# Attention steps in pairs, value scaling in pieces, masks on two engines: one change to a kernel for banded attention and a gated feed-forward block

## The chip, the cores and the metric

The kernel runs on one core of a Trainium2 chip. TensorE (PE) multiplies matrices and its weight loads (PEld) run beside it. VectorE (DVE), ScalarE (ACT) and GpSimd (POOL) do the elementwise work; POOL cannot read the accumulators (PSUM), which PE writes. Transfers are issued from the queues of POOL and SyncE (SP). Each engine takes its instructions in order, so one that waits holds up all that stand behind it. The metric is the device time of one execution in microseconds (us), as the median of several runs.

## The reference

Four batches, eight heads, 768 positions, head width 64. Each query sees the 95 positions before it, itself and the first 8 positions; the scores get a linear bias with one slope per head. The attention output goes through a feed-forward block with 512 inputs and 1536 hidden columns.

```python
scores = scale * np.matmul(q, k.transpose(0, 1, 3, 2))
is_global = pos[None, :] < int(n_global)                  # 8
is_local = (rel >= 0) & (rel < int(n_local))              # 96
bias = -slopes[:, None, None] * dist[None, :, :]
scores = np.where(is_global | is_local, scores + bias[None], -1e9)
a = np.exp(scores - scores.max(-1, keepdims=True))
attn = np.matmul(a / (a.sum(-1, keepdims=True) + 1e-09), v)
x = attn.transpose(0, 2, 1, 3).reshape(B * S, H * D)      # 3072 x 512
g = x @ w_gate
out = (g * (1.0 / (1.0 + np.exp(-g))) * (x @ w_val)) @ w_out
```

## The kernel before

**Attention** is worked for two heads at a time: `Pair(b, hp)` is batch `b` (0 to 3) and head pair `hp` (0 to 3). A pair has six steps, which this text calls by short names. *tr*: 24 PE transposes of q and k into PSUM (`trq`, `trk`), copies on ACT into `qT` and `kT`, and a small copy that puts the 8 global keys into each chunk of `kT` (DVE for batch 0, POOL for the others). *sc0, sc1, sc2*: a third of the keys each, matmuls into two PSUM banks (`scA`, `scB`), two exponentials on ACT into `at`, and two multiplications of `at` with the mask `masks` (DVE for batch 0, POOL for the others). *va0, va1*: half of the queries each; matmuls of `at` with ones (`den`) and with v (`num`), then on DVE a transpose of `den` to `dT`, a reciprocal `dR`, a transpose back that spreads it to `rb`, and last the product with `num` into `xT` (on DVE for batch 0, the "fast" form; else ACT copies `num` to `ns` and POOL multiplies). va0 needs the masked sc0 and sc1; va1 needs sc1 and sc2.

**Feed-forward.** The 3072 tokens are 8 blocks `t` of 384; two blocks are one batch. A block has 12 column groups `f`, and each of these three groups of PE work: gate (`gps`, 4 matmuls), value (`vps`, 4 matmuls) and, from block 1 on, a quarter of an output tile of the block before (`ops`, 3 matmuls). ACT takes the tanh of `gps` into `th`, DVE makes `sl` of `th` and `gps`, then `hT` of `vps` and `sl`. `gps` and `vps` take three PSUM banks in turn (tags x0, x1, x2), `ops` one (o0), which ACT empties into `osb` after every fourth quarter; attention takes four (a0 to a3) in turn. With three banks, the value group of `f+1` uses the bank that `sl` of `f` must have read, and the gate group of `f+2` that of `hT` of `f`.

**What sets the order.** There is no scheduler: each engine's instructions stand in the order in which the code issues them. Half of batch 0 (tr, sc0, sc1, va0 of four pairs) is done ahead, the "prologue". Then the last loop walks the groups and, by a quota of steps for each amount of feed-forward work, calls the next attention step of `plan` between two groups. `second(b)` lists sc2 and va1 of a batch, `first(b)` tr, sc0, sc1 and va0. 80 steps are placed in this way. `loads` says before which group POOL issues the transfers of a later batch: q and k four heads at a time (`load_qk`), v by chunk (`load_v_rest`). After the last block, 12 quarters of `ops` remain.

Of the kernel before, what the change touches and what calls it, by code (L numbers as in the profile page):

```python
# [37 lines left out]
def kernel(  # L38
# [119 lines left out]

    attn_tags = ["a0", "a1", "a2", "a3"]
    pro_tags = ["a0", "a1", "a2", "a3", "x0", "x1", "x2", "o0"]  # L160
    state = {"tags": pro_tags, "n": 0}

    def bank(name, dt=FP32, cols=512):
        tags = state["tags"]
# [5 lines left out]
    def make_masks(h, c0, c1):  # L170
        nc.scalar.activation(
            out=masks[:, h, c0:c1], in_=dist[:, c0:c1], func=AF.Exp, scale=-slopes[h])

    class Pair:
        def __init__(self, b, hp):
# [3 lines left out]
        def transposes(self):  # L179
            b, hp = self.b, self.hp  # L180
            trq = bank("trq", FP16, S)
            trk = bank("trk", FP16, S)
            for st, tr in ((qst[b], trq), (kst[b], trk)):
                for j in range(J):
                    for hi in range(2):
                        nc.tensor.transpose(  # L186
                            tr[64 * hi:64 * hi + 64, 128 * j:128 * j + 128],
                            st[:, 2 * hp + hi, D * j:D * j + D], ident)
            self.qT = sb2.tile([128, S], FP16, name="qT", tag="qT", bufs=NP)
            self.kT = kTs[hp]  # L190
            nc.scalar.copy(
                out=self.qT.rearrange("r (p j) -> r p j", j=J),
                in_=trq.rearrange("r (j p) -> r p j", j=J))
            k3 = self.kT.rearrange("r (c m) -> r c m", m=128)
            t3 = trk.rearrange("r (j p) -> r p j", j=J)
            for c0, c1, n in ((0, 6, KC), (6, 7, S - 6 * KC)):
                nc.scalar.copy(
                    out=k3[:, c0:c1, NG:NG + n].rearrange("r c (p j) -> r c p j", j=J),
                    in_=t3[:, 20 * c0:20 * c0 + (c1 - c0) * (n // J), :].rearrange(
                        "r (c p) j -> r c p j", c=c1 - c0))  # L200
            (nc.vector if b == 0 else nc.gpsimd).tensor_copy(  # L201
                out=k3[:, :, 0:NG],
                in_=k3[:, 0, NG:2 * NG].unsqueeze(1).broadcast_to([128, NCH, NG]))

        def scores(self, bk, mul_eng):
# [10 lines left out]
                        lhsT=self.kT[r, 128 * c:128 * c + 128],  # L216
                        rhs=self.qT[r, q0:q0 + n], start=True, stop=True)
            for hi in range(2):
                keep = f"at{hi}{bk}b{hp}" if bk == 1 else f"at{hi}{bk}"
                at = sb2.tile([128, BANK], FP16, name="at", tag=keep, bufs=1 if "b" in keep else 2)  # L220
                nc.scalar.activation(out=at, in_=sc[hi][:, 0:BANK], func=AF.Exp, scale=scale)  # L221
                self.at[hi, bk] = at
            for hi in range(2):
# [10 lines left out]
        def values(self, half, fast):  # L234
# [11 lines left out]
            for dst, ones_side in ((den, True), (num, False)):  # L246
# [13 lines left out]
            nc.vector.transpose(dT[:, 0:n_q], den[:, 0:n_q])  # L260
            nc.vector.reciprocal(
                out=dR[:, 0:nb], in_=dT[:, 0:n_q].rearrange("p (n i) -> p n i", i=32)[:, :, 0])
            nc.vector.transpose(  # L263
                rb[:, 0:n_q].rearrange("p (n i) -> p n i", i=32),
                dR[:, 0:nb].unsqueeze(2).broadcast_to([128, nb, 32]))
            dst = xT[:, hp, b * S + lo:b * S + hi_q]
            if fast:
                nc.vector.tensor_mul(dst, num[:, 0:n_q], rb[:, 0:n_q])  # L268
            else:
                ns = sb2.tile([128, 416], FP32, name="ns", tag="ns")  # L270
                nc.scalar.copy(out=ns[:, 0:n_q], in_=num[:, 0:n_q])  # L271
                nc.gpsimd.tensor_mul(dst, ns[:, 0:n_q], rb[:, 0:n_q])  # L272


    hTs = {}
# [3 lines left out]
    def gate_or_val(t, f, which):  # L279
        if f == 0 and which == 0:  # L280
            hTs[t] = sb2.tile([128, NFF, TB], FP16, name="hT", tag="hT")
        w = (wg, wv)[which]
        dst = ps.tile([128, 512], FP32, name="gv"[which] + "ps", tag=f"x{gv.get('n', 0) % 3}")
        gv["n"] = gv.get("n", 0) + 1
        for c in range(NC):
            nc.tensor.matmul(  # L286
# [15 lines left out]

    def out_part(t, i, part):
        if part == 0:
            ops_t[0] = ps.tile([128, 512], FP32, name="ops", tag="o0")
        ops = ops_t[0]
        for f in range(3 * part, 3 * part + 3):
            nc.tensor.matmul(  # L308
                ops, lhsT=hTs[t][:, f, 128 * i:128 * i + 128], rhs=wo[:, f, :],
                start=(f == 0), stop=(f == NFF - 1))  # L310
        if part == 3:
            osb = sb2.tile([128, DM], FP32, name="osb", tag="osb")
            nc.scalar.mul(out=osb, in_=ops, mul=0.5)  # L313
            r0 = TB * t + 128 * i
            nc.sync.dma_start(out=out[r0:r0 + 128, :], in_=osb)
# [43 lines left out]
    for t in range(4 + 2 * (NP - 1)):  # L359
        for hp in range(NP):  # L360
            s = t - 2 * hp
            if 0 <= s < 4:
                early(hp, s)
                if s == 1 and hp + 1 < NP:
                    make_masks(2 * hp + 2, 0, BANK)
                    make_masks(2 * hp + 3, 0, BANK)
# [2 lines left out]
    state["tags"] = attn_tags  # L369
    state["n"] = 0  # L370

    def second(b):
        steps = []
        for kind, hp in ((0, 0), (0, 1), (1, 0), (0, 2), (1, 1), (0, 3), (1, 2), (1, 3)):
            p = pairs[b, hp]
            steps.append((lambda p=p: p.values(1, b == 0)) if kind else
                         (lambda p=p: p.scores(2, nc.vector if b == 0 else nc.gpsimd)))
        return steps

    def first(b):  # L380
        keyed = []
        for hp in range(NP):
            p = pairs[b, hp]
            keyed += [(4 * hp, p.transposes),
                      (4 * hp + 2, lambda p=p: p.scores(0, nc.gpsimd)),
                      (4 * hp + 3, lambda p=p: p.scores(1, nc.gpsimd)),
                      (4 * hp + 5, lambda p=p: p.values(0, False))]
        return [fn for _, fn in sorted(keyed, key=lambda x: x[0])]


    plan = [((0,), second(0)), ((1,), first(1)), ((2, 3), second(1) + first(2)),
            ((4, 5), second(2) + first(3)), ((6,), second(3))]

    loads = {13: [lambda: load_qk(1, 4, 8)]}
    for c in range(4, NCH):
        loads[14 + c] = [lambda c=c: load_v_rest(1, c)]
    for b in range(2, B):
        base = 24 * (b - 2) + 26
        loads[base] = [lambda b=b: (stage(b), load_qk(b, 0, 4))]
        loads[base + 2] = [lambda b=b: load_qk(b, 4, 8)]  # L400
        for c in range(NCH):
            loads[base + 3 + c] = [lambda b=b, c=c: load_v_rest(b, c)]


    NT = TOK // TB
# [8 lines left out]
    for blocks, steps in plan:  # L414
# [4 lines left out]
    owed = 0.0  # L419
    seen = set()  # L420
    for t, f, work, fn in groups:
        if (t, f) not in seen:
            seen.add((t, f))
            for ld in loads.get(NFF * t + f, []):
                ld()
        fn()
        owed += work * quota.get(t, 0.0)
        while owed >= 1.0 and todo:
            todo[0][1].pop(0)()
            owed -= 1.0  # L430
            if not todo[0][1]:
                assert t <= todo[0][0]
                todo.pop(0)
                owed = 0.0
    assert not todo
    for i in range(3):
        for part in range(4):
            out_part(NT - 1, i, part)
# [35 lines left out]
```

## Time and profile before

| what | value |
|---|---|
| runs shown: median (lowest to highest) | 285.01 us (284.49 to 285.19) |
| the profiled execution: time, span | 286.0 us, 284.2 us |
| granted TensorE clock | 0.999 |
| DMA queue of POOL | 14.20 MB, 44.3% of 16 engines |

The profiled execution took 1.0 us more than the median of the runs shown; its span, from the first to the last instruction, is 1.8 us less than its own time. All rows below are of this execution, with times from the start of the span. A row of the timeline gives start, duration, engine, line, operation, output and inputs, the number of instructions, and in brackets how long the engine sat idle before it and what ended that. A row of the waits says which line of which engine waited for what: us in total, times, the longest. A row by groups ends with busy time and mean ns, then the idle time ahead of them.

### The profile page before, as it was taken

What the parts mean: (1) busy time and instruction counts of PE and PEld (TensorE: products, weight loads), DVE (VectorE), ACT (ScalarE), POOL (GpSimd) and SP (SyncE); (2) the same over time, 40 slices, a digit from 0 to 9 for tenths busy, and PEclk for the clock granted to TensorE, in tenths of its full rate; (3) what the DMA queues carried; (4) which work ended last, traced back from release to release, by engine and by line L of the source; (5) the groups of instructions that cost most, each with busy time, mean ns of one, the idle gap of its engine ahead of it and who ended that gap; (6) DMA issues with size and microseconds to landing.
All of it is one profiled execution on the core that took longest, in us unless ns stands there. A gap on an engine that the chain in (4) does not pass through costs nothing.

```text
span 284.2 us, 5710 instructions
## 1 busy us (share of the span) xinstructions
PE 258.3 (91%) x2240; PEld 141.4 (50%) x2240; DVE 161.3 (57%) x333; ACT 145.2 (51%) x305; POOL 149.9 (53%) x178
## 2 busy tenths in 40 slices
PE   1687999799988999999999999899999999999973
PEld 1464455444544555545545555555545555555531
DVE  1377589945545576465466666445565676556500
ACT  4788343275654645755754546466655443332211
POOL 8984550067486787873665687694366451000000
PEclk9999999999999999999999999999999999999999
DMA  9999999317070169970000199950100101001011
GB/s 106 169 166 189 203 205 186 26 9 142 3 78 0 39 92 181 97 79 2 37 37 2 39 163 131 87 68 0 39 37 1 39 37 39 24 12 40 38 74 74
DMA packets 45531, 21.28 MB, mean 75 GB/s; under 512 B 28256, under 2 KB 42432, under 8 KB 45504
## 3 DMA queue, kind: packets, MB, share of 16 engines
q0 software_dynamic: 41504, 14.20, 44.3%
q1 hardware_dynamic: 4000, 6.72, 6.5%
q8 instruction: 17, 0.28, 0.4%
q14 instruction: 10, 0.08, 0.1%
HBM read 28.58 MB, written 6.29 MB: 123 GB/s over the span
## 4 chain that ended last, share of the span: by engine, by line
PE 61%; POOL 13%; DMA 13%; issue 7%; ACT 3%; DVE 1%; POOLq 0%; ACTq 0%; DVEq 0%
PE ops L308 20%; PE gps L286 16%; PE vps L286 16%; DMA wo<-in_moe_w_out_dram 4%; POOL at L228 4%; DMA wv<-in_moe_w_val_dram 4%; DMA vS<-in_v_dram 3%; POOL at L232 3%; PE den L250 3%; PE scA L214 3%; PE num L250 2%; DMA qst<-in_q_dram 2%; POOL vS L123 2%; PE trq L186 1%; ACT osb L313 1%
## 5 line engine op out<-in xcount | busy, mean ns | idle before, releaser
L295 DVE SCALAR_TENSOR_TENSOR sl<-th,gps 128x384 f32<-128x384 f32 x96 | 53.0, 552 | 78.3 <-ACT th L293 77.8
L286 PE MATMUL gps<-xT,wg 128*128 128x384 f16 x384 | 80.1, 331 | 2.1 <-DVE xT L268 1.8
L286 PE MATMUL vps<-xT,wv 128*128 128x384 f16 x384 | 79.6, 331 | 1.1 <-DVE sl L295 1.1
L293 ACT ACTIVATE th<-gps 128x384 f32<-128x384 f32 x96 | 47.5, 494 | 64.1 <-PE gps L286 62.6
L308 PE MATMUL ops<-wo,hT 128*128 128x512 f16 x288 | 76.6, 380 | 2.1 <-ACT osb L313 2.1
L299 DVE TENSOR_TENSOR hT<-vps,sl 128x384 f16<-128x384 f32 x96 | 53.2, 554 | 10.0 <-PE vps L286 1.5
L232 POOL TENSOR_TENSOR at<-at,masks 128x432 f16<-128x432 f16 x48 | 47.1, 1001 | 8.1 <-ACT at L221 7.6
L286 PEld LDWEIGHTS <-wg 128*128 128x128 f16 x384 | 35.5, 99 | 31.5 <-issue 3.1
L286 PEld LDWEIGHTS <-wv 128*128 128x128 f16 x384 | 35.9, 98 | 27.0 <-issue 4.2
L272 POOL TENSOR_TENSOR xT<-ns,rb 128x384 f16<-128x384 f32 x24 | 24.0, 998 | 44.7 <-DVE rb L263 28.1
L308 PEld LDWEIGHTS <-hT 128*128 128x128 f16 x288 | 26.0, 98 | 27.3 <-issue 4.9
L221 ACT ACTIVATE at<-scA 128x432 f16<-128x432 f32 x48 | 25.4, 529 | 17.7 <-PE scB L214 16.5
L250 PE MATMUL den<-at,ones 128*64 128x216 f16 (+6 forms) x288 | 19.6, 241 | 6.5 <-POOL at L228 3.2
L221 ACT ACTIVATE at<-scB 128x432 f16<-128x432 f32 x48 | 25.4, 530 | 0.0
L271 ACT COPY ns<-num 128x384 f32<-128x384 f32 x24 | 11.5, 479 | 25.4 <-PE num L250 24.1
L228 POOL TENSOR_TENSOR at<-at,masks 128x432 f16<-128x432 f16 x24 | 23.6, 1005 | 1.5 <-ACT at L221 1.4
L123 POOL DMA_DIRECT2D vS<-in_v_dram x24 | 21.7, 905 | 3.3 <-issue 2.3
L313 ACT ACTIVATE osb<-ops 128x512 f32<-128x512 f32 x24 | 14.4, 599 | 17.0 <-PE ops L308 17.0
L250 PEld LDWEIGHTS <-ones 128*64 128x64 f16 x288 | 12.3, 113 | 19.9 <-issue 14.5
L214 PE MATMUL scA<-qT,kT 64*128 64x216 f16 (+2 forms) x112 | 18.0, 264 | 2.8 <-DVE kT L201 2.7
L260 DVE STREAM_TRANSPOSE dT<-den 128x384 f32<-128x384 f32 x32 | 18.4, 576 | 3.0 <-PE den L250 3.0
L263 DVE STREAM_TRANSPOSE rb<-dR 128x384 f32<-128x384 f32 x32 | 18.5, 578 | 2.7
(32 smaller groups left out, 180.9 us busy)
## 6 DMA issues: line engine op xcount, KB each, us to landing
out_dram<-osb SPq DMA_DIRECT2D x24, 256.0 KB, 2.0
vS<-in_v_dram POOLq DMA_DIRECT2D x20, 120.0 KB, 5.0
qst<-in_q_dram POOLq DMA_DIRECT2D x5, 384.0 KB, 5.4
kst<-in_k_dram POOLq DMA_DIRECT2D x5, 384.0 KB, 6.6
wg<-in_moe_w_gate_dram POOLq DMA_DIRECT2D x4, 384.0 KB, 10.0
wv<-in_moe_w_val_dram POOLq DMA_DIRECT2D x4, 384.0 KB, 10.9
wo<-in_moe_w_out_dram POOLq DMA_DIRECT2D x3, 512.0 KB, 14.2
qst<-in_q_dram POOLq DMA_DIRECT2D x6, 192.0 KB, 6.5
```

Of the source, the lines that this page charges most:

```text
L123: nc.gpsimd.dma_start(out=vSs[b][NG:NG + n, c, :, :], in_=v[b, :, KC * c:KC * c + n, :].rearrange("h p d -> p h d"))
L214: nc.tensor.matmul(sc[hi][:, col:col + n], lhsT=self.kT[r, 128 * c:128 * c + 128], rhs=self.qT[r, q0:q0 + n], start=True, stop=True)
L221: nc.scalar.activation(out=at, in_=sc[hi][:, 0:BANK], func=AF.Exp, scale=scale)
L228: mul_eng.tensor_mul(a2, a2, m[:, WIN:2 * WIN].unsqueeze(1).broadcast_to([128, 2, WIN]))
L232: mul_eng.tensor_mul(at, at, m[:, o:o + BANK])
L250: nc.tensor.matmul(dst[r, o:o + n], lhsT=ones if ones_side else vSs[b][:, c, 2 * hp + hi, :], rhs=self.at[hi, cb][:, col:col + n], start=( ...
L272: nc.gpsimd.tensor_mul(dst, ns[:, 0:n_q], rb[:, 0:n_q])
L286: nc.tensor.matmul(dst[:, 0:TB], lhsT=w[:, c, 128 * f:128 * f + 128], rhs=xT[:, c, TB * t:TB * t + TB], start=(c == 0), stop=(c == NC - 1))
L293: nc.scalar.activation(out=th, in_=dst[:, 0:TB], func=AF.Tanh, scale=0.5)
L295: nc.vector.scalar_tensor_tensor(out=sl, in0=th, scalar=1.0, in1=dst[:, 0:TB], op0=AluOp.add, op1=AluOp.mult)
L299: nc.vector.tensor_mul(hTs[t][:, f, :], dst[:, 0:TB], gv["sl"])
L308: nc.tensor.matmul(ops, lhsT=hTs[t][:, f, 128 * i:128 * i + 128], rhs=wo[:, f, :], start=(f == 0), stop=(f == NFF - 1))
```

## The change

In words, part by part:

- **Pairs.** `plan` now holds lists of steps that are issued directly one behind the other: sc0 with sc1 of the same pair of heads, sc2 of two pairs, va1 of two pairs, tr of two pairs or va0 with tr. Only the steps in block 0 (`single`) and some va0 stay alone. The 80 steps stand in 48 places. `owed` starts at 0.8, and at 0.4 for each new list.
- **Pieces.** The DVE work of a va step is queued as functions in `later`: `invert` (dT and dR), `spread` (rb, and POOL's product) and, for batch 0, `scale_num`. One is run after each feed-forward group; all that are left are run ahead of the next attention place and at each block's start. In the prologue all run at once.
- **Masks.** For batches 1 to 3, sc0 and the sc2 of even pairs multiply on DVE, sc1 and the sc2 of odd pairs on POOL.
- **kT.** Batch 0's two large copies go from ACT to DVE; the copy of the global keys is on DVE for all batches.
- **Banks and buffers.** In block 0 gate and value take four banks (o0 too, which nothing else uses yet). The last three output tiles take a0, a1 and o0. All `at` tags have four buffers.
- **Loads.** q and k of batch 1 (heads 4 to 7) before group 10 instead of 13; of batch 2 before 23 and 24 instead of 26 and 28; of batch 3 before 38 and 40 instead of 50 and 52 (groups are counted 12 to a block); v follows.

```diff
-            (nc.vector if b == 0 else nc.gpsimd).tensor_copy(
+            nc.vector.tensor_copy(
...
+            def invert():
+                nc.vector.transpose(dT[:, 0:n_q], den[:, 0:n_q])
+                nc.vector.reciprocal(
...
+            def spread():
...
+                if not fast:
+                    nc.gpsimd.tensor_mul(dst, ns[:, 0:n_q], rb[:, 0:n_q])
...
+            later.append(invert)
+            later.append(spread)
             if fast:
-                nc.vector.tensor_mul(dst, num[:, 0:n_q], rb[:, 0:n_q])
+                later.append(scale_num)
...
-            ops_t[0] = ps.tile([128, 512], FP32, name="ops", tag="o0")
+            tag = ["a0", "a1", "o0"][i] if t == TOK // TB - 1 else "o0"
...
+    def sc(b, hp, bk):
+        on_vector = b == 0 or bk == 0 or (bk == 2 and hp % 2 == 0)
...
+    def second(b):
+        return [[sc(b, 0, 2), sc(b, 1, 2)], [sc(b, 2, 2), sc(b, 3, 2)],
+                [va(b, 0, 1), va(b, 1, 1)], [va(b, 2, 1), va(b, 3, 1)]]
+    def first(b):
+        return [[tr(b, 0), tr(b, 1)],
+                [sc(b, 0, 0), sc(b, 0, 1)], [sc(b, 1, 0), sc(b, 1, 1)],
+                [va(b, 0, 0), tr(b, 2)], [sc(b, 2, 0), sc(b, 2, 1)],
+                [va(b, 1, 0), tr(b, 3)], [sc(b, 3, 0), sc(b, 3, 1)],
+                [va(b, 2, 0)], [va(b, 3, 0)]]
+    def both(b):
+        x, y = second(b), first(b + 1)
+        return x[:3] + [y[0], x[3]] + y[1:]
+    single = [[sc(0, 0, 2)], [sc(0, 1, 2)], [va(0, 0, 1)], [sc(0, 2, 2)],
+              [va(0, 1, 1)], [tr(1, 0)], [sc(0, 3, 2)], [va(0, 2, 1)], [va(0, 3, 1)], [tr(1, 1)]]
+    plan = [((0,), single), ((1,), first(1)[1:]), ((2, 3), both(1)),
+            ((4, 5), both(2)), ((6,), second(3))]
...
+        if f == 0:
+            run_later(len(later))
+        if t == 1 and f == 0:
+            state["x"] = ["x0", "x1", "x2"]
         fn()
+        run_later(1)
...
-            todo[0][1].pop(0)()
+            run_later(len(later))
+            for step in todo[0][1].pop(0):
+                step()
```

Three places show what moves; the numbers behind the names only tell buffers apart. On DVE in block 0, the rows that follow a va1 step of batch 0, before:

```order
L299 TENSOR_TENSOR hT_480<-vps_651,sl_649 128x384
L260 STREAM_TRANSPOSE dT_679<-den_658 128x384
L261 RECIPROCAL dR_680<-dT_679 128x12
L263 STREAM_TRANSPOSE rb_681<-dR_680 128x384
L268 TENSOR_TENSOR xT_96<-num_657,rb_681 128x384
L295 SCALAR_TENSOR_TENSOR sl_693<-th_691,gps_686 128x384
```

and now:

```order
L317 TENSOR_TENSOR hT_480<-vps_740,sl_738 128x384
L313 SCALAR_TENSOR_TENSOR sl_778<-th_776,gps_771 128x384
L269 STREAM_TRANSPOSE dT_768<-den_747 128x384
L270 RECIPROCAL dR_769<-dT_768 128x12
L317 TENSOR_TENSOR hT_480<-vps_782,sl_778 128x384
L275 STREAM_TRANSPOSE rb_770<-dR_769 128x384
L282 TENSOR_TENSOR xT_96<-num_746,rb_770 128x384
```

The four instructions of the step now let `sl` and `hT` of the next group pass between them. On ACT around the first tr step of batch 2, before (block 2, group f6):

```order
L293 ACTIVATE th_1702<-gps_1697 128x384
L191 COPY qT_1741<-trq_1715 128x768
L197 COPY kT0_76<-trk_1716 128x6x120
L197 COPY kT0_76<-trk_1716 128x48
L293 ACTIVATE th_1752<-gps_1747 128x384
```

and now (block 2, group f1):

```order
L311 ACTIVATE th_1545<-gps_1540 128x384
L198 COPY qT_1575<-trq_1549 128x768
L204 COPY kT0_76<-trk_1550 128x6x120
L204 COPY kT0_76<-trk_1550 128x48
L198 COPY qT_1606<-trq_1580 128x768
L204 COPY kT1_77<-trk_1581 128x6x120
L204 COPY kT1_77<-trk_1581 128x48
L311 ACTIVATE th_1626<-gps_1621 128x384
```

Two pairs' copies now stand between two tanh, and the step comes five groups `f` earlier. On POOL around the transfers of q and k of batch 2, before:

```order
L232 TENSOR_TENSOR at_1500<-at_1500,masks_73 128x432
L232 TENSOR_TENSOR at_1502<-at_1502,masks_73 128x432
L112 DMA qst_1506<-in_q_dram 128x4x384
L112 DMA kst_1507<-in_k_dram 128x4x384
L272 TENSOR_TENSOR xT_96<-ns_1556,rb_1552 128x384
L232 TENSOR_TENSOR at_1588<-at_1588,masks_73 128x432
```

and now:

```order
L238 TENSOR_TENSOR at_1360<-at_1360,masks_73 128x432
L238 TENSOR_TENSOR at_1362<-at_1362,masks_73 128x432
L238 TENSOR_TENSOR at_1415<-at_1415,masks_73 128x432
L238 TENSOR_TENSOR at_1417<-at_1417,masks_73 128x432
L112 DMA qst_1430<-in_q_dram 128x4x384
L112 DMA kst_1431<-in_k_dram 128x4x384
L112 DMA qst_1430<-in_q_dram 128x4x384
```

The transfers stand behind the masks of the last sc2 steps of batch 1, issued at block 1, groups f8 and f10, and ahead of the first tr of batch 2 by only two groups `f`.

More of the change, by code (lines that the diff above doesn't have):

```diff
@@ L391, with va, tr @@
-    plan = [((0,), second(0)), ((1,), first(1)), ((2, 3), second(1) + first(2)),
-            ((4, 5), second(2) + first(3)), ((6,), second(3))]
-    loads = {13: [lambda: load_qk(1, 4, 8)]}
+    def sc(b, hp, bk):
+        on_vector = b == 0 or bk == 0 or (bk == 2 and hp % 2 == 0)
+        return lambda: pairs[b, hp].scores(bk, nc.vector if on_vector else nc.gpsimd)
+    def va(b, hp, half):
+        return lambda: pairs[b, hp].values(half, b == 0)
+    def tr(b, hp):
+        return pairs[b, hp].transposes
@@ L433 @@
                 todo.pop(0)
-                owed = 0.0
-    assert not todo
+                owed = 0.4
+    assert not todo and not later
     for i in range(3):
```

54 lines of the change are left out of this document (23 added, 31 removed).

## The prediction

> **What bounds the kernel now.** First the busy times: PE is busy nearly all the span, the others little more than half.
>
> ```profile
> PE 258.3 (91%) x2240; PEld 141.4 (50%) x2240; DVE 161.3 (57%) x333; ACT 145.2 (51%) x305; POOL 149.9 (53%) x178
> ```
>
> So the time is PE's work plus what it waits, and two views say where a gain can be. The waits of PE in three stretches (block 0, blocks 1 to 6, the end) name the stalls:
>
> ```profile
> PE gps L286 <- DVE xT L268: 1.8, 2, 1.2
> PE vps L286 <- DVE sl L295: 1.1, 2, 0.7
> PE gps L286 <- DVE hT L299: 0.3, 1, 0.3
> ...
> PE den L250 <- POOL at L228: 3.2, 7, 0.7
> PE num L250 <- DMA vS<-in_v_dram: 1.5, 2, 1.0
> ...
> PE ops L308 <- ACT osb L313: 2.1, 3, 0.7
> ```
>
> The second is PE's timeline, read by the distance from start to start. In steady flow a group of the feed-forward takes 0.65 us (89.66, 90.31, 90.96):
>
> ```profile
> 89.66 0.82 PE L308 MATMUL ops<-wo,hT 128*128 128x512 f16 x3
> 90.31 0.81 PE L286 MATMUL gps<-xT,wg 128*128 128x384 f16 x4
> 90.96 0.81 PE L286 MATMUL vps<-xT,wv 128*128 128x384 f16 x4
> 91.71 0.26 PE L214 MATMUL scA<-qT,kT 64*128 64x216 f16 x1
> ...
> 92.00 0.82 PE L308 MATMUL ops<-wo,hT 128*128 128x512 f16 x3
> ```
>
> But the value group ahead of an attention step (here sc2) takes 0.75, so entering costs 0.10. The step's 432 columns, at the pace of a group's 4 x 384 in 0.65, should take 0.18; it takes 0.29, so leaving costs 0.10 or a little more. No wait stands there. In the prologue sc1 stands directly behind sc0 (the third row begins it), and starts stay 0.18 apart across the border; only the exit to the transposes is longer (0.32):
>
> ```profile
> 9.13 0.38 PE L214 MATMUL scA<-qT,kT 64*128 64x216 f16 x1
> ...
> 9.31 0.38 PE L214 MATMUL scA<-qT,kT 64*128 64x216 f16 x1
> ...
> 9.49 0.38 PE L214 MATMUL scA<-qT,kT 64*128 64x216 f16 x1
> ...
> 9.81 0.85 PE L186 MATMUL trq<-ident,qst 128*64 128x128 f16 x12
> ```
>
> Like steps side by side pay neither.
>
> **The change, part by part.**
>
> *Pairs.* 80 places become 48; each of the 32 merged steps keeps its tile shape (64*128 twice, or 128*64 twice), and saves 0.20: 32 x 0.20 = -6.4. Lower bound of the gain: only the exit, -3.2.
>
> *Waits that go.* sc0's masks (POOL at L228), va's wait for them 3.2 in 7 times: on DVE a mask takes 378 ns, on POOL 1005, and two places now lie between them and va0.
>
> ```profile
> L232 DVE TENSOR_TENSOR at<-at,masks 128x432 f16<-128x432 f16 x16 | 5.5, 378 | 1.3 <-ACT at L221 1.2
> L228 POOL TENSOR_TENSOR at<-at,masks 128x432 f16<-128x432 f16 x24 | 23.6, 1005 | 1.5 <-ACT at L221 1.4
> ```
>
> 24 sc0 masks and 12 of sc2 leave POOL (36 us of its 149.9), so v's transfers, which stood behind them, land early: 1.5. At the end the last three output tiles have banks of their own, so nothing waits for `osb`: 2.1.
>
> ```profile
> 270.79 2.75 PE L308 MATMUL ops<-wo,hT 128*128 128x512 f16 x12 [0.69 <-ACT osb L313]
> 274.22 2.75 PE L308 MATMUL ops<-wo,hT 128*128 128x512 f16 x12 [0.69 <-ACT osb L313]
> ```
>
> These two start 3.43 apart; 12 matmuls at 0.65 for three take 2.60. A wait shown as 0.69 costs 0.83, 0.14 more (drain and refill). With 12 such waits: 3.2 + 1.5 + 2.1 + 12 x 0.14 = 8.5. Bounds -6.8 to -9.5; I take -8.5.
>
> *Block 0.* Here DVE is the bound, not PE:
>
> ```profile
> 37.60:56.60 19.00, 16.32 (x185) 9.99 (x184) 17.58 (x39) 6.19 (x15) 3.67 (x4) 1.00 1.08 134
> ```
>
> The fifth number (17.58) is DVE's: of 19.0 us from 37.6, with its issue gaps, all. Pieces take nothing away:
>
> ```profile
> 38.78 0.57 DVE L260 STREAM_TRANSPOSE dT<-den 128x384 f32<-128x384 f32 x1
> ...
> 40.81 0.55 DVE L295 SCALAR_TENSOR_TENSOR sl<-th,gps 128x384 f32<-128x384 f32 x1
> ```
>
> The four instructions of a va hold DVE for 2.03 us from `dT` to the next `sl`, before and after. With four banks and earlier va, DVE begins this stretch some 2 us sooner, but a pair of masks of batch 1 (0.76) is new ahead of `hT` of f11, and `num` is held until the last piece, which keeps the a-banks. Walked in this order with these durations, block 1's first gate group ends near 57.9, with two tr and four sc already done that came behind it before. Before, that group ends where the first tr begins:
>
> ```profile
> 55.93 0.53 PE L186 MATMUL trq<-ident,qst 128*64 128x128 f16 x12
> ...
> 56.72 0.82 PE L286 MATMUL vps<-xT,wv 128*128 128x384 f16 x4
> ```
>
> A tr takes 0.79, an sc 0.29 and each entry 0.10: 2 x 0.89 + 4 x 0.39 = 3.3, of which 0.4 is counted under pairs. 55.9 + 3.3 - 0.4 - 57.9: +0.9 gained, so -0.9. Bounds -3 (the three DVE waits above gone) to +2. The transfers set a floor: k for the first tr of batch 1 lands at 29.49 + 12.4 = 41.9, for the second at 35.62 + 13.6 = 49.2; PE gets there near 42 and 51, so little is waited.
>
> ```profile
> 29.49 0.70 POOL L112 DMA_DIRECT2D kst<-in_k_dram  x1
> ...
> DMA to landing us min/median/max: 12.4/12.4/12.4
> ...
> 35.62 0.70 POOL L112 DMA_DIRECT2D kst<-in_k_dram  x1 [1.23 <-DMA wg<-in_moe_w_gate_dram]
> ...
> DMA to landing us min/median/max: 13.6/13.6/13.6
> ```
>
> *Prologue.* kT's large copy takes 0.77 on ACT, where q's copy stands ahead of it; on DVE it runs beside that one, but behind two masks and ahead of the va work of the pair before. No row has it on DVE; ACT's own duration is the nearest. One gain and one delay of the same size: I take 0, with one copy hidden or added as bounds, -0.8 to +0.8.
>
> ```profile
> L197 ACT COPY kT<-trk 128x720 f16<-128x720 f16 x16 | 12.3, 772 | 0.6 <-PE trk L186 0.6
> ```
>
> *At no cost.* Four buffers for every `at`: no row of PE or ACT waits for one. The loads of batch 3 are issued nine groups `f` (18 us at 3 x 0.65 each) ahead of their first tr, so they land under it; if the queue were late they would add to (a). SP only issues the output tiles behind `osb`, in the same order.
>
> *New waits.* (a) k of batch 2. From the last sc2 place of block 1 (f10, its start is 0): after a tanh (0.6) four exponentials, 0.42 apart, end at 2.4; POOL's two masks (1.96 together) begin with the third and end at 4.0; q is issued then, k 0.8 later, and k lands up to 6.6 after that:
>
> ```profile
> 85.27 1.96 POOL L232 TENSOR_TENSOR at<-at,masks 128x432 f16<-128x432 f16 x2
> ...
> 86.27 0.53 ACT L221 ACTIVATE at<-scA 128x432 f16<-128x432 f32 x1 [0.65 <-PE scB L214]
> ...
> 86.69 0.52 ACT L221 ACTIVATE at<-scB 128x432 f16<-128x432 f32 x1
> ...
> L112 POOL DMA_DIRECT2D kst<-in_k_dram x1: 766/766/766, 62.1 to 62.1; - x1
> ...
> DMA to landing us min/median/max: 5.4/6.0/6.6
> ```
>
> That is 11. PE gets to the k transposes after 9 groups (5.9), the scores (0.6) and two va1 (4 x 744 columns, 1.3, with 0.2 at the border) plus the q half (0.4): 8.4. Stall +2.5, bounds 0 and 4.
>
> (b) Bursts. The gate group of 90.31 ends at 90.96, and `sl` of it at 92.25, 1.29 later; the value group that needs the bank comes 3 x 0.65 = 1.95 later. Slack 0.66, plus any step between.
>
> ```profile
> 91.69 0.56 DVE L295 SCALAR_TENSOR_TENSOR sl<-th,gps 128x384 f32<-128x384 f32 x1 [0.67 <-ACT th L293]
> ```
>
> Four exponentials fit in it. Two tr do not where no step follows at once, at the end of block 3: from 0.5 on (0 is their start) their copies hold ACT for 2 x 1.45 us (111.52 to 112.96), tanh and `sl` end at 4.5, and PE, after 1.5 for the tr and four groups, wants the bank at 4.1: 0.4. The copy of global keys now waits on DVE for ACT's kT: at the end of block 2 it comes 2.7 after the start of va0 and tr, a whole va0 (invert and spread, 1.55) stands behind it and ahead of `sl`, which ends at 4.8 where PE wants 4.0: 0.8. Two va1 twice within two groups `f` at the end of block 5 leave 0.5 in block 6. Elsewhere the PE time of the next step covers it. Sum +1.7, bounds 0 and 6.
>
> ```profile
> 111.52 0.80 ACT L191 COPY qT<-trq 128x768 f16<-128x768 f16 x1 [1.27 <-PE trq L186]
> ...
> 112.96 0.52 ACT L293 ACTIVATE th<-gps 128x384 f32<-128x384 f32 x1
> ```
>
> (c) DVE masks beside POOL's. No row of before shows this: batch 0's DVE masks ran while POOL only issued transfers. Nearest from below is no loss (DVE's `hT`, at 85.46 beside POOL's masks, took its usual 0.56); from above each of 18 pairs of masks waits for a running POOL pair, 1.96. Within a step DVE's masks come 0.8 ahead of POOL's, so most miss each other: if one in four is caught, 18 x 1.96 / 4 = 8.8 on DVE, and the slack of 0.66 and the steps' own PE time take most of it. I take +1.5, near the lower end, since the nearest row is the undisturbed one; the upper end is rival 4.
>
> ```profile
> 85.46 0.56 DVE L299 TENSOR_TENSOR hT<-vps,sl 128x384 f16<-128x384 f32 x1
> ```
>
> The Trainium skill speaks against the change here: its page "SBUF — State Buffer", section "Who interferes with whom", says that a VectorE instruction with two SBUF inputs and a GpSimd one that reads SBUF exclude each other for a whole instruction, while one with a single SBUF input is not held. The undisturbed `hT` (one input in PSUM) agrees; a mask has both inputs in SBUF. By the rule the upper end of (c) can be met.
>
> *Sum*: -6.4 - 8.5 - 0.9 + 0 + 2.5 + 1.7 + 1.5 = -10.1. The span goes from 284.2 to 274.1, the profiled execution from 286.0 to 275.9, the median (285.0, 1.0 below that execution) to 274.9.
>
> **Rivals.**
> 1. *Everything new is covered*: (a), (b) and (c) at their lower ends, 285.0 - 15.8 = 269.2, with a rest 271. For it: no other engine is above 60%. Against: in-order ACT and DVE with 0.66 of slack.
> 2. *Like steps drain too* (the pairs don't save): 274.9 + 6.4 = 281.3. Against it stand the even 0.18 of the prologue.
> 3. *DVE becomes the bound in bursts*: masks add 36 x 0.378 = 13.6 us to it and global keys 12 x 0.34, to about 180 of 275 us. If (b) and block 0 come at their upper ends: 274.9 + 4.3 + 2.9 = 282.1.
> 4. *Slower*: DVE masks that wait for POOL's. 18 pairs x 1.96 = 35.3 us on DVE, in order ahead of `sl` or `hT`; less 18 x 0.66 of slack, 23.4 reach PE: 285.0 - 11.6 + 23.4 = 296.8. It decides from 0.6 us per pair of masks at PE (11.6 / 18), a delay of 1.3 on DVE. For it: nothing in the order keeps the two engines' masks apart. Against: the 0.8 between them.
>
> **How the numbers follow.** Chances: forecast 0.62, rival 1 0.16, rival 2 0.07, rival 3 0.08, rival 4 0.07 (0.04 of it beyond the point where it decides). 0.3%, or 0.9 us, is about what a measurement can tell from no change. Faster by more 0.93, within it 0.03, slower 0.04. The range 269.5 to 281.0 takes in the forecast's unknown costs and half of rival 1; 0.8 of the chance lies in it.
>
> **What would show it.** PE: no wait of `den` for L228, of `num` for vS, of `ops` for `osb`; entries of 0.10 only once for a pair of steps. POOL's busy time near 111 us, DVE's near 180. PE's first `trq` of batch 2 (block 2, f1) should wait for a transfer of q or k for 2 to 3 us. In block 0 DVE should be busy without a gap to near 58. DVE masks above 378 ns, or gaps ahead of them, beside POOL's masks would show rival 4; more than 0.18 (0.10 at full clock) between two scores steps side by side, rival 2. The forecast is wrong if PE's waits for `sl` in blocks 1 to 5 sum to over 6 us, or if block 1 begins later than 60.

## The result and the profile after

The changed kernel takes 276.19 us (median; 274.74 to 276.4) where the kernel before takes 284.85 (284.49 to 285.19): ratio 0.9685, interval 0.965 to 0.9721. The forecast was 274.9. The profiled execution took 276.11 with a span of 274.3; the forecast for the span was 274.1.

The busy times of the page, to be set against those of before:

```profile
PE 250.5 (91%) x2240; PEld 143.3 (52%) x2240; DVE 179.6 (65%) x389; ACT 141.4 (52%) x297; POOL 113.4 (41%) x130
```

DVE's 179.6 and POOL's 113.4 are what was forecast (near 180 and 111). PE's share is unchanged, so PE still bounds the kernel. The list of PE's waits has lost `den` for POOL's masks, `num` for vS and `ops` for `osb`. Of its rows, the two for q and k and those for `xT` ahead of attention steps are new or longer; the `den` row is that of the prologue (1.4 before), and `sl` has the same sum as before at other places (block 0 then, 126.03 and 156.58 now):

```profile
PE trq L193 <- DMA qst<-in_q_dram: 8.1, 3, 5.9
PE trk L193 <- DMA kst<-in_k_dram: 3.0, 3, 2.2
PE den L256 <- DVE at L238: 1.8, 1, 1.8
PE vps L304 <- DVE sl L313: 1.1, 2, 0.7
PE trq L193 <- DVE xT L282: 0.7, 1, 0.7
PE scA L221 <- DVE xT L282: 0.3, 1, 0.3
```

The longest of the first row (5.9) is the start of the program, and 0.4 of the second is in the prologue too. The rest is in two places of PE's timeline: the first tr of batch 1, and the two tr of batch 2 side by side.

```profile
41.89 0.53 PE L193 MATMUL trq<-ident,qst 128*64 128x128 f16 x12 [1.36 <-DMA qst<-in_q_dram]
42.87 0.53 PE L193 MATMUL trk<-ident,kst 128*64 128x128 f16 x12 [0.46 <-DMA kst<-in_k_dram]
...
91.30 0.81 PE L304 MATMUL gps<-xT,wg 128*128 128x384 f16 x4
92.94 0.53 PE L193 MATMUL trq<-ident,qst 128*64 128x128 f16 x12 [0.83 <-DMA qst<-in_q_dram]
95.64 0.53 PE L193 MATMUL trk<-ident,kst 128*64 128x128 f16 x12 [2.17 <-DMA kst<-in_k_dram]
```

At the end, 36 matmuls of three output tiles follow the last quarter of the block before (3 more) without a gap, 39 in one row:

```profile
261.62 8.58 PE L327 MATMUL ops<-wo,hT 128*128 128x512 f16 x39
```

To see where the time went, I took PE's distances from start to start from the first feed-forward group on, took off 0.65 per group, the step's own pace and 0.09 for an entry, and summed what is left wherever it is over 0.12. These "other losses" are 16.0 us before and 13.3 after, at 80 and 48 places of attention: the waits that the forecast named are gone, 9.2 of the 16.0, but what there is besides has grown from 6.8 to 13.3. The experiments ask which.

### The profile page after: what moved, and what is told of

It is laid out like the page before. It is cut to its first block, busy times and chain, and to the rows that moved or that the text cites. A ratio compares the mean times of both kernels' runs of the same rounds, so it can differ in the third digit from the quotient of the medians.

```text
span 274.3 us, 5703 instructions
## 1 busy us (share of the span) xinstructions
PE 250.5 (91%) x2240; PEld 143.3 (52%) x2240; DVE 179.6 (65%) x389; ACT 141.4 (52%) x297; POOL 113.4 (41%) x130
## 4 chain that ended last, share of the span: by engine, by line
PE 70%; DMA 13%; DVE 5%; POOL 5%; ACT 3%; issue 2%; DVEq 0%; ACTq 0%; POOLq 0%
PE ops L327 21%; PE vps L304 19%; PE gps L304 19%; DMA kst<-in_k_dram 9%; DMA wv<-in_moe_w_val_dram 4%; PE den L256 3%; PE scA L221 3%; PE num L256 2%; POOL qst L112 1%; POOL vS L117 1%; PE trk L193 1%; DVE rb L275 1%; DVE sl L313 1%; DVE dT L269 1%; DVE hT L317 1%
## 5 line engine op out<-in xcount | busy, mean ns | idle before, releaser
L313 DVE SCALAR_TENSOR_TENSOR sl<-th,gps 128x384 f32<-128x384 f32 x96 | 52.3, 545 | 44.7 <-ACT th L311 44.6
L317 DVE TENSOR_TENSOR hT<-vps,sl 128x384 f16<-128x384 f32 x96 | 52.5, 547 | 8.4 <-PE vps L304 1.8
L279 POOL TENSOR_TENSOR xT<-ns,rb 128x384 f16<-128x384 f32 x24 | 24.0, 1001 | 72.0 <-DVE rb L275 63.7
L304 PEld LDWEIGHTS <-wg 128*128 128x128 f16 x384 | 36.3, 99 | 32.8 <-issue 2.0
L327 PEld LDWEIGHTS <-hT 128*128 128x128 f16 x288 | 27.1, 98 | 24.8 <-issue 0.7
L234 POOL TENSOR_TENSOR at<-at,masks 128x432 f16<-128x432 f16 x24 | 24.8, 1053 | 13.5 <-ACT at L227 13.2
L238 DVE TENSOR_TENSOR at<-at,masks 128x432 f16<-128x432 f16 x52 | 26.7, 540 | 1.3 <-ACT at L227 1.2
L227 ACT ACTIVATE at<-scB 128x432 f16<-128x432 f32 x48 | 26.1, 544 | 0.0
L256 PE MATMUL den<-at,ones 128*64 128x216 f16 (+6 forms) x288 | 18.0, 240 | 2.9 <-DVE at L238 1.8
L290 ACT COPY ns<-num 128x384 f32<-128x384 f32 x24 | 11.5, 478 | 15.9 <-PE num L256 14.0
L193 PE MATMUL trq<-ident,qst 128*64 128x128 f16 x192 | 9.5, 244 | 8.8 <-DMA qst<-in_q_dram 8.1
```

Of the source, the lines that this page charges most:

```text
L234: mul_eng.tensor_mul(a2, a2, m[:, WIN:2 * WIN].unsqueeze(1).broadcast_to([128, 2, WIN]))
L238: mul_eng.tensor_mul(at, at, m[:, o:o + BANK])
L256: nc.tensor.matmul(dst[r, o:o + n], lhsT=ones if ones_side else vSs[b][:, c, 2 * hp + hi, :], rhs=self.at[hi, cb][:, col:col + n], start=( ...
L304: nc.tensor.matmul(dst[:, 0:TB], lhsT=w[:, c, 128 * f:128 * f + 128], rhs=xT[:, c, TB * t:TB * t + TB], start=(c == 0), stop=(c == NC - 1))
L313: nc.vector.scalar_tensor_tensor(out=sl, in0=th, scalar=1.0, in1=dst[:, 0:TB], op0=AluOp.add, op1=AluOp.mult)
L317: nc.vector.tensor_mul(hTs[t][:, f, :], dst[:, 0:TB], gv["sl"])
```

## The experiments

Medians in us; each ratio is to the kernel before on the same chip. The runs from flat to kT change the changed kernel. Best joins three of these edits, and the last four change best.

| run | what is different | median | ratio | interval |
|---|---|---|---|---|
| changed kernel | | 276.19 | 0.9685 | 0.965 to 0.9721 |
| flat | pairs undone | 275.73 | 0.9677 | 0.9656 to 0.9698 |
| masks | shared masks undone | 280.18 | 0.9823 | 0.9797 to 0.9849 |
| load 2 | q, k of batch 2 earlier | 272.07 | 0.9549 | 0.9529 to 0.9569 |
| fast | product of va on DVE for all | 297.76 | 1.0446 | 1.042 to 1.0472 |
| q, k of batch 1 | issued earlier | 276.17 | 0.9698 | 0.9676 to 0.9719 |
| no clearing | pieces go on over a block's start | 276.36 | 0.9685 | 0.9655 to 0.9715 |
| kT | batch 0's copies on ACT again | 277.22 | 0.9734 | 0.9713 to 0.9755 |
| best | load 2 + q, k of batch 1 + no clearing | 270.76 | 0.951 | 0.9489 to 0.9531 |
| best, flat | pairs undone | 275.68 | 0.9666 | 0.9637 to 0.9695 |
| best, masks | shared masks undone | 270.5 | 0.9485 | 0.9453 to 0.9516 |
| best, once | pieces undone, all batches | 269.45 | 0.9452 | 0.9425 to 0.948 |
| best, three banks | fourth bank in block 0 undone | 270.72 | 0.9502 | 0.9473 to 0.9531 |

### Pairs, alone and with transfers in time

```diff
     for blocks, steps in plan:
+        steps = [[s] for group in steps for s in group]
```

> The changed kernel (276.2 us, span 274.3) with every attention step alone again, in the same order: 80 places instead of 48, nothing else. Theory (like steps side by side save one entry and one exit, 0.20 us): +6.4 for 32 places; against it the first tr of batch 2 comes two groups f later, so its wait for q and k (3.0 us of PE in the changed kernel) goes, and so do most of the bursts (about 1.5): 276.2 + 6.4 - 3.0 - 1.5 = 278 us, and PE starts show 0.74 to 0.75 ahead of each of the 80 steps. Rival (the pairs save nothing, the time came from the waits that went): 276.2 - 4.5 = 271.7 us.

275.73: neither 278 nor 271.7. Flat, PE has 80 entries again and 5.9 us of other losses, not 13.3. What the pairs save in entries they give back in waits that only the paired order has. The largest is the one for q and k of batch 2: flat, POOL issues k at 88.34, half a microsecond earlier than in the changed kernel (88.83), but PE comes to the first tr of batch 2 at 96.62, and not near 92.1 as in the paired order (92.94 less its wait of 0.83), and waits for nothing:

```profile
88.83 0.76 POOL L112 DMA_DIRECT2D kst<-in_k_dram  x1
```

```profile
88.34 0.75 POOL L112 DMA_DIRECT2D kst<-in_k_dram  x1
...
96.62 0.53 PE L193 MATMUL trq<-ident,qst 128*64 128x128 f16 x12
```

The first row is the changed kernel's, the others are of the flat one.

So a second test had to take that wait away first. In the following run q and k of batch 2, with v behind them, are issued at block 1's group f8, not f11:

```diff
-    for b, base, step in ((2, 23, 1), (3, 38, 2)):
+    for b, base, step in ((2, 20, 1), (3, 38, 2)):
```

It leaves out the transfer of the last 48 positions of v of batch 1 (0.69 us of POOL's time), whose place in the list the edit overwrites.

> The changed kernel with q, k and v of batch 2 issued three groups f earlier (before group 20 instead of 23). Theory (PE waits 0.83 and 2.17 us for q and k because POOL issues them behind two steps' masks, only two groups f ahead): the wait goes, 276.2 - 3.0 = 273.2 us, span near 271.3. Rival (the wait only moves: POOL's masks of sc2 come 1.6 us later behind the issues, and va1 of batch 1 waits for them): 275.5 to 276.5 us.

272.07, 4.1 below the changed kernel. The tr of batch 2 wait for nothing, and PE's other losses fall from 13.3 to 9.4: 3.2 of that stood at this place, and 0.7 comes from a q of batch 1 that landed earlier in this execution. Term (a) is thereby shown.

```profile
91.34 0.53 PE L193 MATMUL trq<-ident,qst 128*64 128x128 f16 x12
91.70 0.50 PE L193 MATMUL trk<-ident,kst 128*64 128x128 f16 x12
```

The best version has all of v and three edits (the other two are told below). On it the pairs were undone once more.

> The best version so far (270.76), with the pairs undone: 80 single places in the same order. It repeats the first experiment where no wait for q and k of batch 1 or 2 can hide what the pairs bring. Theory A (the pairs save 32 x 0.20 = 6.4 in entries and exits, and give back some 2 to 3 in bursts that are left, since the flat one had 5.9 of other losses and the best one has 7.5): 273.5 to 275. Theory B (pairs bring nothing, as 275.73 against 276.19 seemed to say): 270.5 to 271.

275.68: theory A, a little over its range. The four medians stand in a square: flat 275.73 with late loads and 275.68 with early ones, paired 276.19 and 270.76 (the early side also has the edit to the pieces). The edits to the loads alone bring nothing, pairs alone bring nothing, both together bring 5. From the first feed-forward group the flat version takes 246.6 us (274.1 - 27.49) and the paired one 241.3 (268.5 - 27.24), with other losses of 5.9 and 7.5 (1.7 apart before rounding): entries and exits cost 5.3 + 1.7 = 7.0 more, 0.22 for each of 32 merged steps, where 0.20 was forecast. PE's timeline of the changed kernel shows why: a second sc2 (198.38) starts 0.03 behind the last matmul of the first, 48 columns wide, with no stop at the border, and two steps take 0.48 to the next group.

```profile
198.18 0.26 PE L221 MATMUL scA<-qT,kT 64*128 64x216 f16 x1
...
198.35 0.18 PE L221 MATMUL scA<-qT,kT 64*128 64x48 f16 x1
...
198.38 0.25 PE L221 MATMUL scA<-qT,kT 64*128 64x216 f16 x1
...
198.66 0.82 PE L304 MATMUL vps<-xT,wv 128*128 128x384 f16 x4
```

### Masks on one engine or two

```diff
-        on_vector = b == 0 or bk == 0 or (bk == 2 and hp % 2 == 0)
+        on_vector = b == 0
```

> The changed kernel with all masks of batches 1 to 3 on POOL again (36 instructions back from DVE). Theory (sc0 on DVE is what took the waits of den for its masks away, 3.2 us and refill in the kernel before): PE waits for POOL's masks again, but two places now lie between sc0 and va0, so about half: +2 us, and POOL 36 us busier delays q and k of batch 2 by another 2 us: 280 us. DVE's masks fall back to 0.38 us each. Rival (DVE masks that wait for POOL cost more than they save): below 276.2, near 275.

280.18 as expected, but of the two reasons given only the second came true. `den` did not wait for POOL's masks; POOL came later to q and k, behind eight masks in a row, and PE stood at the same tr. The waits there are 5.0, not 3.0, and PE then ran at half pace (last section):

```profile
83.73 7.74 POOL L238 TENSOR_TENSOR at<-at,masks 128x432 f16<-128x432 f16 x8
91.41 0.83 POOL L112 DMA_DIRECT2D qst<-in_q_dram  x1
...
96.34 0.85 PE L193 MATMUL trq<-ident,qst 128*64 128x128 f16 x12 [3.87 <-DMA qst<-in_q_dram]
98.31 0.85 PE L193 MATMUL trk<-ident,kst 128*64 128x128 f16 x12 [1.12 <-DMA kst<-in_k_dram]
```

The same edit on the best version:

> The best version so far (270.76), with all masks of batches 1 to 3 on POOL again. Theory A (what masks on DVE brought was that POOL comes to the transfers of q and k in time, 4.0 us at 280.18 against 276.19; with these issued early they bring nothing, and the masks that VectorE and GpSimd hold up for each other, about 1 us at PE, are gone): 269.8 to 271, DVE 378 ns for a mask of batch 0 and no others. Theory B (PE waits for POOL's masks at the den matmuls, as before, 3.2 plus 7 x 0.14): 274 to 275.

270.5: theory A. Its list of waits still has no `den` behind a mask of POOL. The 3.2 us that PE waited for those masks before did not go because DVE does masks; what is left as the cause is above all the new order, with one or two places of other steps between sc1 and va0, where there was one or none. The line that PE waited for (L228) is moreover that of sc1's masks, which POOL does before and after. Nor does `num` wait for vS in this run or the one before it, so v did not need the 36 us that masks on DVE spare POOL; what is left there is that the change issues the transfers of batches 2 and 3 earlier.

### The product of va, and who holds up DVE's masks

In the changed kernel the masks on DVE are slower than the 378 ns of before, and POOL's slower than 1005:

```profile
L234 POOL TENSOR_TENSOR at<-at,masks 128x432 f16<-128x432 f16 x24 | 24.8, 1053 | 13.5 <-ACT at L227 13.2
L238 DVE TENSOR_TENSOR at<-at,masks 128x432 f16<-128x432 f16 x52 | 26.7, 540 | 1.3 <-ACT at L227 1.2
```

Of 18 pairs of DVE masks of batches 1 to 3, 8 took more than 1 us, the others about the 0.76 of an undisturbed pair. Seven of the eight stand, in the timelines of POOL and DVE, at POOL's product of a va (L279) and the POOL masks right behind it, which are drawn out too (1.96 undisturbed):

```profile
165.01 1.00 POOL L279 TENSOR_TENSOR xT<-ns,rb 128x384 f16<-128x384 f32 x1 [0.87 <-DVE rb L275]
165.97 2.24 POOL L234 TENSOR_TENSOR at<-at,masks 128x432 f16<-128x432 f16 x2
...
165.23 2.12 DVE L238 TENSOR_TENSOR at<-at,masks 128x432 f16<-128x432 f16 x2
```

The eighth has only POOL's masks beside it:

```profile
56.61 4.23 POOL L234 TENSOR_TENSOR at<-at,masks 128x432 f16<-128x432 f16 x4 [7.65 <-ACT at L227]
...
58.49 1.47 DVE L238 TENSOR_TENSOR at<-at,masks 128x432 f16<-128x432 f16 x2
```

Taken one by one, 11 DVE masks last 1.0 to 1.2. Five of them start up to 0.22 behind the start of a product, six up to 0.22 behind that of a POOL mask.

If the product holds the masks up, or brings POOL's masks to where they do, moving it to DVE must bring the masks back:

```diff
-        return lambda: pairs[b, hp].values(half, b == 0)
+        return lambda: pairs[b, hp].values(half, True)
```

> The changed kernel with the product into xT of batches 1 to 3 on DVE, straight from num, as for batch 0: 24 products leave POOL and 24 copies leave ACT, DVE gains 24 x 0.48 = 11.5 us. Theory (a DVE mask and a running POOL operation exclude each other; in the changed kernel 8 of 18 pairs of DVE masks took 1.46 to 2.12 us instead of 0.76, nearly always beside POOL's product): the DVE masks of batches 1 to 3 fall to 0.76 a pair in nearly all places, 8 us of DVE time; with the banks held one group longer the time stays within 1.5 us of 276.2. Rival (the masks are long for another reason, as the wait for the exponentials): pairs of 1.46 to 2.12 us stay, and the time rises by 2 us or more.

The masks came back, the time did not stay. A DVE mask takes 394 ns on the mean and one pair of 18 is over 1 us, beside POOL's masks (57.68). The run does not tell the product from POOL's masks, which come at other times without it. And it takes 297.76: with the product read from `num` the bank is held until the last piece has run, and the scores wait for that bank (14.6 of the 21.6 us that are new; two more rows for `xT` have 2.5 and 1.5):

```profile
L238 DVE TENSOR_TENSOR at<-at,masks 128x432 f16<-128x432 f16 x52 | 19.4, 394 | 3.5 <-ACT at L227 3.1
...
PE scA L221 <- DVE xT L282: 14.6, 13, 2.1
```

My expectation had costed only DVE's time, not the life of the bank.

### Pieces

Once more on the best version:

```diff
                 nc.scalar.copy(out=ns[:, 0:n_q], in_=num[:, 0:n_q])
+            run_later(len(later))
```

> The best version so far (270.76), with the pieces undone for batches 1 to 3: transpose, reciprocal and spread are issued at once behind the va step. Block 0 keeps its pieces. A whole va0 holds DVE for 1.55. Theory A (slack is 0.66 plus the step's own 0.7 of PE, so a single va is covered to about 0.2, but two va1 together are 3.1 against 2.1): six places of two va1 cost about 1 each, those with tr and the copy of the global keys 0.5 each: 275 to 278. Theory B (DVE has room, pieces only move the work): 270.5 to 271.5.

269.45, the fastest of all runs, below both theories and with no overlap with best (270.37 to 271.25) or three banks (270.27 to 271.38), on the same chip. Undoing the pieces is a gain of 1.3. But the added line stands behind both branches, so batch 0 loses its pieces too, unlike what the expectation says, and the gain has to be told apart by blocks. In the profiled executions (spans 268.5 and 267.5) block 1 begins at 54.95, not 55.60, though the feed-forward starts 0.82 later (28.06). Block 1 then takes 1.08 longer, since its first output quarter waits for `hT`, which stands on DVE behind a pair of masks of 1.98, held up beside POOL's:

```profile
57.80 0.81 PE L328 MATMUL ops<-wo,hT 128*128 128x512 f16 x3 [1.38 <-DVE hT L318]
```

Blocks 2, 4 and 6 are shorter by 0.30, 0.88 and 0.24. One thing that changed is the row of the masks (lines behind L290 are one higher in this kernel):

```profile
L234 POOL TENSOR_TENSOR at<-at,masks 128x432 f16<-128x432 f16 x24 | 23.8, 1010 | 31.0 <-ACT at L227 31.0
L238 DVE TENSOR_TENSOR at<-at,masks 128x432 f16<-128x432 f16 x52 | 20.8, 420 | 2.3 <-ACT at L227 2.0
```

420 ns, where the best version has 555; two pairs of 18 over 1 us, not nine. The pieces put `spread`, which releases POOL's product, directly ahead of the next place, which is often a scores step, and so POOL works just as DVE's masks come. At once behind the va, the product is done before. The masks are not the whole reason, though, since with all of them on POOL best gained only 0.3. Of the 0.88 in block 4, 0.50 goes with a wait of `scB` for the bank of `den`, which `invert` frees late when it is queued. That wait stands in best and, as this row shows, in best, masks too:

```profile
158.95 0.25 PE L221 MATMUL scB<-qT,kT 64*128 64x216 f16 x1 [0.25 <-DVE dT L269]
```

The other 0.37 stands behind a pair of DVE masks of 2.12. Both are gone without pieces. What the gains in blocks 2 and 6 and ahead of block 1 consist of was not separated. PE's other losses fall from 7.5 to 5.8.

### Three places of block 0 and its border

q and k of batch 1 ahead of the output weights:

```diff
-    load_wo(0)
     load_qk(1, 0, 2)
+    load_wo(0)
     load_wo(1)
-    load_wo(2)
     load_qk(1, 2, 4)
+    load_wo(2)
```

> One thing changes: in the prologue POOL issues q and k of batch 1 for heads 0 and 1 ahead of the first part of the output weights, and those for heads 2 and 3 ahead of the last part, not behind. In the changed kernel PE came to the first tr of batch 1 at about 40.5, waited for q (1.36 shown) and k (0.46), some 2.1 us lost from start to start. Theory A (the landing of q and k is what holds block 0 there): that wait goes, and the median falls by 1.5 to 2.1 us, to 274.1 to 274.7. Theory B (DVE is the bound of block 0, so PE only waits for DVE instead): block 1's first gate group still ends near 57.9 and the median stays within 0.6 of 276.2.

276.17, but not by theory B: the wait at 41.89 is gone and block 1's first gate group ends at 56.66, not 57.93. The 1.3 us were lost again at batch 2, where PE waited 0.94 and 2.11, in sum as long as in the changed kernel, and then ran at half pace (last section); block 2 took 1.7 longer.

```diff
-        if f == 0:
-            run_later(len(later))
```

> One thing changes: the pieces that are left over at a block's start are not all run there, but go on one after each group. It touches the starts of blocks 2 and 3 alone (three and two pieces). In the changed kernel PE waited 0.85 at the start of block 3, where a whole va0 and the copy of the global keys stand on DVE ahead of sl. Theory A (that order on DVE is what PE waits for, as predicted under bursts): the 0.85 goes, the median falls by 0.6 to 1.0 us. Theory B (the wait is only moved, since DVE has the same work to do in those groups): within 0.3 us of the changed kernel.

The wait at the start of block 3 went, as theory A has it. In the changed kernel PE waits for `sl`, which stands behind kT's copy and a whole va0 on DVE (first rows, gate and value of group f1); without the clearing the same two groups pass (second rows), and the block takes 29.7, not 30.5:

```profile
126.03 0.81 PE L304 MATMUL gps<-xT,wg 128*128 128x384 f16 x4
127.53 0.81 PE L304 MATMUL vps<-xT,wv 128*128 128x384 f16 x4 [0.69 <-DVE sl L313]
```

```profile
127.43 0.81 PE L304 MATMUL gps<-xT,wg 128*128 128x384 f16 x4
128.08 0.81 PE L304 MATMUL vps<-xT,wv 128*128 128x384 f16 x4
```

The median stayed (276.36), as the profiled execution lost about 2 us more than the changed kernel at batch 2's tr: 2.51 for k, and the half pace. A single run of these kernels thus moves by what happens there, and small edits can't be read from their times.

All three edits to loads and pieces together:

> The changed kernel with three edits that the runs so far point to: q and k of batch 2 are issued three groups f earlier (all of v loaded), q and k of batch 1 ahead of the output weights, and no clearing of the queue of pieces at a block's start. The first alone gave 272.07. If the three add up: 272.1 - 0.85 - 1.5 to 2.1, so 269.2 to 269.8. If block 0 is bound by DVE and the second edit gives nothing: 271.2. If the pieces' wait is only moved too: 272.1.

270.76, 1.3 below load 2 alone (1.1 by the ratios, as the chips differ), so about half of the two small gains arrived. The fourth bank was then undone on it (`x0, x1, x2` from the start):

> The best version so far (270.76), with three banks for gate and value in block 0, not four. Theory A (DVE is the bound of block 0, as the prediction has it, so that a fourth bank only lets PE run ahead): block 1 begins within 0.4 of where it did, the median is 270.6 to 271.2. Theory B (PE runs into the bank that sl or hT still holds whenever pieces stand ahead of them): block 1 begins 1.5 to 3 later, 272.3 to 273.8.

270.72: theory A; the fourth bank brings nothing.

```diff
-                (nc.vector.tensor_copy if b == 0 else nc.scalar.copy)(
+                nc.scalar.copy(
```

> One part undone: batch 0's two large copies of k go back to ACT. In the changed kernel the feed-forward began at 27.24, 0.76 earlier than before (28.00), which the prediction put at 0 with bounds of 0.8 both ways. Theory A (the copy on DVE beside q's copy on ACT shortens the prologue): the feed-forward begins near 28.0 again, and the span is longer by about 0.8. Theory B (the gain comes from something else, as the queue of pieces or the earlier masks): it begins near 27.2 still. A point aside: since the first tr of batch 1 then waits for q and k in any case, the 0.8 may not reach the end; then the start moves and the median stays within 0.3.

In between: the feed-forward begins at 27.64 (27.24 with the copies on DVE, 28.00 before), and the median rose by 1.0, with intervals of the ratios that just overlap. It begins between 27.17 and 28.09 in the runs that leave the copies on DVE, so 0.4 is inside what that start moves by itself, and the share of kT's copies in the 0.76 stays open.

## Why the prediction was right, and where its terms were not

The sum was right (span 274.3 against 274.1), with terms that were not all right. Pairs, waits and (c) came out better than forecast, (a) and (b) worse, by 0.6 to 1.2 each; that these misses nearly cancel is luck.

- *Pairs, -6.4.* 7.0 in entries and exits on the best version. In the changed kernel itself nothing of it reached the end, since the pairs moved the tr of batch 2 ahead of its transfers and made bursts. The forecast had the parts in separate terms, and so came out right.
- *Waits that go, -8.5.* All three are gone; from start to start they had cost 9.2. The cause given for the first was wrong: L228 is the line of sc1's masks, not of sc0's, and PE does not wait for it with all masks on POOL either. The same runs go against the cause given for the second, the time that POOL gains.
- *Block 0, -0.9.* The gate group ends at 57.93, as walked (57.9). But "so little is waited" for q and k failed: PE came to the first tr at 40.5, not 42, and k landed at 42.9, not 41.9; 2.1 us were lost from start to start, and DVE, which the forecast had busy without a gap, stood idle there and after it (gaps of 1.24, 0.49 and 0.84). With that wait gone the group ended at 56.66, so DVE was not what held the block to 57.9, and that the walk met the end to 0.03 is luck. Of the 2.1, 0.76 was made up by the earlier start of the feed-forward; which row of the walk was too long by the rest was not separated.
- *Prologue, 0.* It was -0.76, within the bounds of 0.8, on their side of a gain.
- *(a) +2.5.* The size was 3.2 here, and more in runs in which half pace followed. The mechanism (k behind the masks of POOL) is shown by load 2 and masks.
- *(b) +1.7.* The three places named cost 0.85 (start of block 3), 0.59 (end of block 3) and 0.23 (block 6), where 0.8, 0.4 and 0.5 were forecast. Some 1.2 more (0.50 at 163.27, 0.37 at 166.86, 0.28 at 105.48) was not foreseen, and it is gone in the run without pieces.
- *(c) +1.5.* "One in four caught" was 8 of 18, and it cost DVE (540 - 378) x 52 = 8.4 us, near the 8.8. PE lost little of that: with all masks on POOL the best version is 0.3 faster, less than its interval. Beside the drawn-out masks stand POOL's masks (six of eleven), which rival 4 spoke of, and its product of va (five), which the prediction left out. The row that stood for this (an undisturbed `hT` beside POOL's masks) could not show it.

Of the rivals, the first did not come true for the changed kernel. After three more edits, which take (a) away, the times reach its range (270.76 and 269.45 lie in 269.2 to 271), but waits for `sl` and `hT` are still there. Rival 2 is refuted by the square, rival 3 by the bursts, which came to 2.9 of its 6.0, and by block 0. Rival 4's mechanism is there, at a price that PE hardly sees: 0.37 where it can be read (166.86).

## What to carry to other kernels

When steps are moved closer together, a transfer that was in time before may not be: compute for each load what its queue does ahead of the issue and when the new order reads it, and move the issue in the same change. An edit whose gain ends in a wait looks worthless alone (pairs, 0) and shows its worth once the wait is gone (pairs, 5); so test parts on the version without the wait. Work cut in pieces is late by its pieces: ask what each piece releases, beside what that will run, and which bank it holds.

## What the chip showed that was not expected

**A wait can cost more than itself.** After the wait for q and k of batch 2, the granted clock fell to half in some executions. Two rows of the same stretch (the column behind POOL's is the clock), the first of the changed kernel, the second of no clearing:

```profile
96.60:97.90 1.30, 1.30 (x17) 0.71 (x12) 0.18 (x1) 1.30 (x4) 0.00 (x0) 1.00 1.32 200
```

```profile
96.60:97.90 1.30, 1.30 (x8) 0.58 (x5) 0.18 (x1) 1.30 (x4) 0.18 (x1) 0.50 1.33 202
```

In the second PE's groups then start 1.26 and 1.28 apart, not 0.65:

```profile
96.68 1.46 PE L304 MATMUL vps<-xT,wv 128*128 128x384 f16 x4
97.94 1.49 PE L327 MATMUL ops<-wo,hT 128*128 128x512 f16 x3
```

That costs 1.2 us or more, on top of the wait. The same half pace stands at the start of the feed-forward in both kernels (gate and value groups 1.28 apart at 30.02 before, 1.25 at 29.88 now), so it does not part them. The column reads 1.00 over 27.24 to 32.00 before and 0.50 now, so the distance from start to start is the better witness of the two. At batch 2 the fall was seen with waits of 1.00 and 2.51 (no clearing), 0.94 and 2.11 (q, k of batch 1), 0.84 and 1.70 (kT) and 3.87 and 1.12 (masks), and not with 0.83 and 2.17 in the changed kernel's profile, so the length alone does not decide. The Trainium skill, page "TensorE: Matmul & The Clock Gate", section "Part 1: The HAM clock gate", says that the clock falls to half after an idle window of about 3.4 us, and that the windows run freely, so that it depends on where one lies. The free window agrees with the mixed outcome; a whole idle window is more than was needed here, as in kT the longest single gap ahead of the fall was 1.70.

**VectorE and GpSimd hold each other up.** The page "SBUF — State Buffer" of the Trainium skill, section "Who interferes with whom", has the rule that the prediction cited. The trace agrees in two ways: DVE masks (two SBUF inputs) beside a GpSimd product and masks took up to 2.12 for a pair that takes 0.76, and in the run in which all but one pair have neither beside them a mask takes 394 ns. That both sides grow (POOL's pair from 1.96 to 2.24) is a thing I had put to one side only.
